# Two spectral-mixing and gated layers on one core: the order of down products, a staging buffer for row forms, and smaller issue pieces in the woven transforms

## The chip, the core and the metric

The kernel runs on one core of a Trainium2 chip. The metric is the time of one execution on the device, in microseconds; lower is better. Before the change the median of three runs is 1369.7 us (1366.79 to 1371.06).

## What is computed

An input x of 2048 rows by 512 columns, in float32, goes through two layers. Each layer has two residual steps: a spectral filter over both axes and a gated unit whose two branches are multiplied without a nonlinearity. Both begin with a layer normalization.

```python
x = x + irfft2(rfft2(layernorm(x)) * (w_r + 1j * w_i))
h = (layernorm(x) @ w_gate) * (layernorm(x) @ w_up)
x = x + h @ w_down
```

There are 2048 x 257 filter coefficients, and w_gate and w_up are 512 x 1792, w_down 1792 x 512; both layers use the same weights.

## The kernel before

**Data.** x stays in SBUF for the whole kernel as `xs`, 16 tiles of 128 x 512. A float32 operand that TensorE is to multiply at full accuracy in its reduced format is split into a high and a low part (`hi`/`lo`, `split`: a cast on ScalarE, then a subtraction), and one product becomes three matmuls, high x high, high x low, low x high (`mm3`, line 107).

**The stages of a layer.** A forward transform (`fwd_steps`, line 215) takes each tile through steps a0 (sums and differences, twiddle load), a1 (transposes), a2 (row transform) and a3 (column part into the buffer `E`). `mid_phase` does the rest of the column transform, the filter and the way back. `inv_steps` (line 382) brings each tile back by b0 (twiddle load), b1 (product `vp` out of `E`, split into `vs`) and b2 (twelve matmuls `yi`, three additions to xs, then the deviation for the next normalization). `stats` and `rstd` compute mean and deviation: `rstd` issues the square root on ScalarE and leaves four small VectorE operations in the list `small`, which `fill` issues at some later place.

**Forms.** The gated unit multiplies with a Strassen-like scheme in seven products, so it wants sums and differences of blocks, of the rows and of the weights. `build_x` (line 430) makes the row forms of a pair of tiles: `norm` (normalize), `turn` (four transposes into a bank `tq`, twice), `forms` (copies and sums, high and low parts of `XA`, three blocks, and of `XS`, four blocks). `XA` and `XS` hold 512 columns, that is one half of the rows. `beside` makes the weight forms (`wt`, from the loaded `rg`) of the next slice of 128 hidden columns on ScalarE and GpSimd, and the split of its down weights (`wd`, from `rw`), distributed over the seven products of the running unit by the list `names`.

**A unit** (`unit`, line 529) is one slice `ft` for one half of the rows (512 columns) or for half of that (256 columns, called a half unit here). Its products, in the order of issue, are p5 (bank `gw`), p1 (`gx`), p6 (`gy`), p2 (adds onto `gx`), p7 (`gz`), p3 (`gv`), p4 (adds onto `gz`): six matmuls each. VectorE combines the banks into c12 and c21, and `split` makes h of each, on ScalarE and GpSimd. The down products of a unit (`down`, three matmuls into one of two banks `db`, then an addition to xs on VectorE) are not issued in the unit itself but handed on as `prev` and issued between the products of the next unit: eight for a full unit, four for a half one. With the shares `(0, 0, 0, 3, 8, 8, 8)` of eight, three come after p2 and five after p7.

**Order.** From the first unit of a layer to the end of its last one, every engine executes instructions in the order of issue (`pin`, line 111). So the order in the program is the order of the queues: SyncE's for the loads of `rg`, `rw` and twiddles, GpSimd's for the low parts and sums, VectorE's and ScalarE's for everything that leaves a bank. `weave` (line 622) mixes a list `side` into a list `main`: each entry has a cost, and after each entry of main so many entries of side are issued that the shares of both sums keep pace, with the side ending at the fraction `frac` of main. Entries of main marked `hold` are followed by none. A side entry of cost 0 is issued together with the one before it as soon as its turn comes.

**One layer's gated units** (line 685 on), with the pinned order: half units (0, 1) of the first 256 columns with the rest of the inverse transform woven in; half units (0, 1) of the other 256 columns; the ten full units 2 to 11 with the second half's inverse (`inv2`) woven in; then half units 12 and 13, beside which the row forms of the second half replace those of the first in `XA` and `XS`, half by half; the ten full units 11 to 2 of the second half, in the first layer with the next forward transform (`fa`) woven in; half units 1 and 0.

**Buffers.** `E` (tag "e", one buffer) is read last by b1 of the last tile and written again by the next forward transform. The five buffers of tag "g" hold `rw`, `vs`, `xn`, `fo`, `fe`, `us` in turn, a new tenant waiting for the old one's last reader. PSUM has the banks x, y, w (one each), a (three: transforms and transposes) and d (two: down products).

## Time and profile before

| | |
|---|---|
| median of three runs | 1369.7 us (1366.79 to 1371.06) |
| the profiled execution, its time | 1371.37 us |
| its span, first to last instruction | 1369.6 us |
| busy in that span: TensorE matmuls | 1199.9 us (88%), 5804 instructions |
| weight loads (beside the matmuls) | 945.9 us (69%) |
| VectorE | 901.1 us (66%) |
| GpSimd | 765.3 us (56%) |
| ScalarE | 468.4 us (34%) |
| mean granted TensorE clock | 0.956 |

PE is TensorE, PEld its weight loads, DVE VectorE, ACT ScalarE, POOL GpSimd, SP SyncE. In a row of groups stand line, engine, operation, output and inputs by the program's names, shape and count, then busy time and mean duration in ns, then the idle time of the engine in front of them and what ended it. Line 123 is the helper that records every operation, so groups are told apart by their tiles. A busy PE is not PE at its peak, since the ends of matmuls are modelled; distances between starts are the safer measure. In rows of a timeline the first numbers are start and length in us, and brackets hold the idle time before.

### The profile page before, as it was taken

To read this page: it belongs to the slowest core of one execution; us is meant where nothing else is said; L and a number is where in the kernel's file an instruction comes from. 1 tells how busy PE (TensorE), PEld (TensorE's weight loads), DVE (VectorE), ACT (ScalarE), POOL (GpSimd) and SP (SyncE) were. 2 spreads that over 40 slices of the span, in tenths; PEclk is the share of its full clock that TensorE was granted. 3 is DMA by queue.
4 is the path that set the end of the run, shared out by engine and by line. 5 is a ranking of instruction groups with operands and counts; after the bars stand their busy time and mean duration, and the time that the engine had idled before them with its cause. 6 is when DMAs were issued, how large, how long until landed. Compare 5 with 4: busy or idle time off the path is not lost.

```text
span 1369.6 us, 16523 instructions
## 1 busy us (share of the span) xinstructions
PE 1199.9 (88%) x5804; PEld 945.9 (69%) x5804; DVE 901.1 (66%) x1669; ACT 468.4 (34%) x947; POOL 765.3 (56%) x804
## 2 busy tenths in 40 slices
PE   5888569999998978989989885699999989999998
PEld 4736557777777756777777365577777777777777
DVE  8568446666668776655576684466766687566666
ACT  5965223222322333333325652232222322322221
POOL 4443338655774655756651333385557745877772
PEclk9989789999999989999999897899999999999999
DMA  5531001111200010112104310011111012211011
GB/s 220 185 138 40 16 8 51 54 43 54 72 33 9 1 47 27 54 50 67 42 16 170 128 49 8 16 47 54 46 39 50 32 43 70 69 47 46 31 32 62
DMA packets 30754, 77.67 MB, mean 57 GB/s; under 512 B 3408, under 2 KB 11856, under 8 KB 28368
## 3 DMA queue, kind: packets, MB, share of 16 engines
q1 hardware_dynamic: 29952, 73.54, 15.8%
q0 software_dynamic: 288, 2.10, 0.5%
q8 instruction: 46, 0.75, 0.2%
q10 hardware_dynamic: 432, 0.98, 0.2%
q14 instruction: 36, 0.29, 0.1%
HBM read 72.42 MB, written 4.19 MB: 56 GB/s over the span
## 4 chain that ended last, share of the span: by engine, by line
PE 53%; DVE 22%; POOL 12%; issue 7%; ACT 4%; DMA 1%; POOLq 0%; SPq 0%; DVEq 0%; ACTq 0%
PE db L123 13%; DVE xs L123 10%; PE gx L123 9%; PE gz L123 8%; PE gw L123 4%; PE gy L123 4%; PE gv L123 4%; DVE q L123 3%; PE yi L123 3%; POOL wt L123 3%; PE dp L123 2%; POOL jz L123 2%; PE sp L123 2%; DVE st L123 2%; PE vp L123 2%
## 5 line engine op out<-in xcount | busy, mean ns | idle before, releaser
L123 PE MATMUL db<-wd,h 128*128 128x512 f32 x1344 | 378.1, 408 | 42.1 <-DVE xs L123 30.9
L123 DVE TENSOR_TENSOR xs<-xs,db 128x512 f32<-128x512 f32 x448 | 304.2, 685 | 106.6 <-PE db L123 105.9
L123 PEld LDWEIGHTS db<-wd,h 128*128 128x128 f32 x1344 | 235.2, 189 | 141.5 <-DVE xs L123 101.9
L123 POOL TENSOR_TENSOR wt<-rg,wt 128x512 fp32r<-128x512 f32 (+1 forms) x216 | 232.8, 1085 | 135.7 <-ACT wt L123 134.8
L123 POOL TENSOR_TENSOR h<-q,h 128x512 fp32r<-128x512 f32 (+1 forms) x144 | 167.9, 1185 | 167.5 <-ACT h L123 167.5
L123 PE MATMUL gx<-xA,wt 128*128 128x512 f32 (+1 forms) x864 | 189.2, 356 | 5.8 <-ACT s L123 5.6
L123 ACT CAST wt<-rg 128x512 fp32r<-128x512 f32 (+1 forms) x216 | 110.6, 539 | 183.3 <-POOL rg L123 168.4
L123 PEld LDWEIGHTS gx<-xA,wt 128*128 128x128 f32 x864 | 144.2, 197 | 28.5 <-ACT s L123 10.5
L123 ACT CAST h<-q 128x512 fp32r<-128x512 f32 (+1 forms) x144 | 75.6, 525 | 233.5 <-DVE q L123 232.6
L123 POOL TENSOR_TENSOR rg<-rg 128x256 f32<-128x256 f32 x200 | 147.6, 738 | 10.7
L123 PE MATMUL gw<-xS,wt 128*128 128x512 f32 (+1 forms) x432 | 97.6, 359 | 43.3 <-ACT xS L123 22.3
L123 DVE TENSOR_TENSOR q<-gy,s 128x512 f32<-128x512 f32 (+1 forms) x72 | 41.2, 572 | 139.9 <-PE gy L123 55.9
L123 POOL TENSOR_TENSOR wd<-rw,wd 128x512 fp32r<-128x512 f32 x52 | 69.0, 1328 | 85.7 <-ACT wd L123 85.7
L123 PEld LDWEIGHTS gw<-xS,wt 128*128 128x128 f32 x432 | 72.1, 195 | 60.4 <-ACT xS L123 23.9
L123 PE MATMUL gy<-xS,wt 128*128 128x512 f32 (+1 forms) x432 | 93.9, 355 | 0.0
L123 POOL TENSOR_TENSOR sx<-sx 128x256 f32<-128x256 f32 x64 | 47.7, 745 | 78.9 <-ACT sx L123 75.1
L123 PE MATMUL gz<-xS,wt 128*128 128x512 f32 (+1 forms) x432 | 90.8, 346 | 0.6 <-DVE q L123 0.6
L123 PE MATMUL gv<-xS,wt 128*128 128x512 f32 (+1 forms) x432 | 91.2, 347 | 0.0
L123 PE MATMUL gz<-xA,wt 128*128 128x512 f32 (+1 forms) x432 | 90.4, 346 | 0.0
L123 PEld LDWEIGHTS gz<-xS,wt 128*128 128x128 f32 x432 | 72.8, 190 | 13.9 <-DVE q L123 1.0
L123 PEld LDWEIGHTS gv<-xS,wt 128*128 128x128 f32 x432 | 72.9, 192 | 12.8
L123 PEld LDWEIGHTS gy<-xS,wt 128*128 128x128 f32 x432 | 73.0, 199 | 9.3
(88 smaller groups left out, 1619.0 us busy)
## 6 DMA issues: line engine op xcount, KB each, us to landing
rg<-in_wb_dram SPq DMA_DIRECT2D x50, 512.0 KB, 3.5
rw<-in_wb_dram SPq DMA_DIRECT2D x52, 256.0 KB, 2.6
wq<-in_wf_dram SPq DMA_DIRECT2D x10, 1024.0 KB, 4.8
wr<-in_wf_dram SPq DMA_DIRECT2D x6, 1024.0 KB, 5.6
tw<-in_tf_dram SPq DMA_DIRECT2D x32, 128.0 KB, 2.1
tw<-in_ti_dram SPq DMA_DIRECT2D x32, 128.0 KB, 2.1
out_dram<-xs SPq DMA_DIRECT2D x16, 256.0 KB, 2.0
xs<-in_x_dram SPq DMA_DIRECT2D x7, 512.0 KB, 7.9
```

The lines of the kernel that those rows point to most:

```text
L123: ins = f(*args, **kw)
```

## The change

Six things are changed.

- **Down products.** The shares become `(0, 0, 2, 4, 6, 8, 8)`: two downs each after p6, p2, p7 and p3 (one each in a unit that follows a half unit). Those after p3 are held like p3 itself. The split of c12 is issued after the downs behind p3 instead of inside p3, and the split of the down weights (`dh`, `dl`) after p4 instead of after p7.
- **Row forms of the second half.** `norm`, `turn` and the four sums are woven into the ten full units and the first half unit of slice 12, and written to a buffer `xf` of tag "e" (the place of `E`) of eight blocks for each pair; for the half units that follow, copies (`high`) and differences (`low_a`, `low_s`) from there into `XA` and `XS` remain. In layer 0 a new `E` is taken after that. The blocks of `XA` are in another order, with the products' indices to match.
- **Inverse.** b2's additions become entries b3 and b4 of their own, then `stats`, `rstd`, and its four small operations (`rest`) one step later; building of row forms starts one step later (`n + 4`), and the inverse's steps before the pinned order reach one further (`< 9`).
- **Forward.** `stats` and a0 get cost 0.2, and `rest` is an entry of its own, one step after `rstd`; `fill` is gone.
- **Weaves.** The fractions become 0.8 (from 1.0) for the first half units, 0.93 (from 0.7) for the long one, 0.6 (from 0.7) for the two that build row forms.
- **Half unit 12** of the first half belongs to the long weave.

```diff
@@ -176,28 +176,24 @@
...
 
-    small = []
-
-    def fill(n=1):
-        for _ in range(min(n, len(small))):
-            small.pop(0)()
-
     def rstd(nm):
...
         A.activation(q, var, AF.Sqrt, bias=eps)
-        small.extend([
-            lambda: V.reciprocal(r0, q),
-            lambda: stt(q, var, EPS, r0, op0=ALU.add, op1=ALU.mult),
-            lambda: stt(q, q, -0.5, r0, op0=ALU.mult, op1=ALU.mult),
-            lambda: stt(r, q, 1.5, r0, op0=ALU.add, op1=ALU.mult)])
+
+        def rest():
+            V.reciprocal(r0, q)
+            stt(q, var, EPS, r0, op0=ALU.add, op1=ALU.mult)
+            stt(q, q, -0.5, r0, op0=ALU.mult, op1=ALU.mult)
+            stt(r, q, 1.5, r0, op0=ALU.add, op1=ALU.mult)
+
+        nm["rest"] = rest
         nm["r"] = r
...
     def normed(t, nm):
-        fill(9)
         xn = temp("xn", "g")
@@ -231,7 +227,6 @@
...
             tt(fe[:, 1], fo[:, 2], fo[:, 3], ALU.subtract)
-            fill(9)
 
@@ -264,7 +259,6 @@
...
                 A.mul(u[64:128, jj, 1:256], dp[q, 257:512], r[q])
-                fill()
 
@@ -278,12 +272,13 @@
...
             ts = nms[t]["ts"]
-            ops.append((n, 4, 0, lambda t=t: stats(t, nms[t])))
+            ops.append((n, 4, 0.2, lambda t=t: stats(t, nms[t])))
             if t == ts[-1]:
                 ops.append((n, 5, 0, lambda t=t: rstd(nms[t])))
+                ops.append((n + 1, 5, 0.1, lambda t=t: nms[t]["rest"]()))
             i = ts.index(t)
             b = n - i + len(ts) + i
-            for d, f, o, c in ((0, a0, 3, 0), (1, a1, 2, 0.43), (2, a2, 6, 1.3), (4, a3, 1, 0.9)):
+            for d, f, o, c in ((0, a0, 3, 0.2), (1, a1, 2, 0.43), (2, a2, 6, 1.3), (4, a3, 1, 0.9)):
                 ops.append((b + d, o, c, lambda f=f, t=t: f(t)))
@@ -409,25 +404,33 @@
...
                         i == 0, i == 3)
-            xt = xs[:, t].rearrange("p (a d) -> p a d", a=2)
+            s["y"] = yp
+
+        def b3(t):
+            xt, yp = xs[:, t].rearrange("p (a d) -> p a d", a=2), S[t]["y"]
             tt(xt, xt, yp[:, None, 0:256].to_broadcast([128, 2, 256]), ALU.add)
+
+        def b4(t):
+            xt, yp = xs[:, t].rearrange("p (a d) -> p a d", a=2), S[t]["y"]
             tt(xt[:, 0], xt[:, 0], yp[:, 256:512], ALU.add)
             tt(xt[:, 1], xt[:, 1], yp[:, 256:512], ALU.subtract)
-            stats(t, nms[t])
-            if t == nms[t]["ts"][-1]:
-                rstd(nms[t])
-            s.clear()
+            S[t].clear()
 
...
         for n, t in enumerate(order):
-            for d, f, o, c in ((0, b0, 3, 0), (1, b1, 2, 1.0), (2, b2, 4, 1.42)):
+            nm = nms[t]
+            for d, f, o, c in ((0, b0, 3, 0), (1, b1, 2, 1.0), (2, b2, 4, 1.42), (2, b3, 5, 0.3), (2, b4, 6, 0.3)):
                 ops.append((n + d, o, c, lambda f=f, t=t: f(t)))
+            ops.append((n + 2, 7, 0.3, lambda t=t: stats(t, nms[t])))
+            if t == nm["ts"][-1]:
+                ops.append((n + 2, 8, 0, lambda nm=nm: rstd(nm)))
+                ops.append((n + 3, 3, 0.1, lambda nm=nm: nm["rest"]()))
             if build and n % 2:
-                for k, (c, f) in enumerate(build(nms[t])):
-                    ops.append((n + 3 + k // 2, 5 if k < 2 else 1, c, f))
+                for k, (c, f) in enumerate(build(nm)):
+                    ops.append((n + 4 + k // 2, 9, c, f))
         return in_steps(ops)
 
-    def build_x(X, nm, tags):
+    def build_x(X, nm, tags, stage=None):
 
@@ -443,24 +446,46 @@
...
             s[h] = tq.rearrange("p (b k s) -> p b k s", b=2, k=2)
+            if stage is not None:
+                A.copy(stage["t"][:, r, 2 - 2 * h:4 - 2 * h], s[h])
 
...
             A.copy(S[:, 0:2], b)
-            A.copy(XA[:, 0:2, 0, :, cols], a)
-            A.copy(XA[:, 2, 0, :, cols], b[:, 1])
+            A.copy(XA[:, 1:3, 0, :, cols], a)
+            A.copy(XA[:, 0, 0, :, cols], b[:, 1])
             gtt(S[:, 1], S[:, 0], S[:, 1], ALU.add)
...
             gtt(S[:, 3], S[:, 3], S[:, 2], ALU.subtract)
-            tt(XA[:, 0:2, 1, :, cols], a, f32(XA[:, 0:2, 0, :, cols]), ALU.subtract)
-            tt(XA[:, 2, 1, :, cols], b[:, 1], f32(XA[:, 2, 0, :, cols]), ALU.subtract)
+            tt(XA[:, 1:3, 1, :, cols], a, f32(XA[:, 1:3, 0, :, cols]), ALU.subtract)
+            tt(XA[:, 0, 1, :, cols], b[:, 1], f32(XA[:, 0, 0, :, cols]), ALU.subtract)
             A.copy(XS[:, :, 0, :, cols], S)
...
 
+        def sums():
+            G_ = stage["t"][:, r]
+            gtt(G_[:, 5], G_[:, 0], G_[:, 1], ALU.add)
+            gtt(G_[:, 4], G_[:, 2], G_[:, 0], ALU.subtract)
+            gtt(G_[:, 6], G_[:, 5], G_[:, 2], ALU.subtract)
+            gtt(G_[:, 7], G_[:, 3], G_[:, 6], ALU.subtract)
+
+        def high():
+            A.copy(XA[:, :, 0, :, cols], stage["t"][:, r, 1:4])
+            A.copy(XS[:, :, 0, :, cols], stage["t"][:, r, 4:8])
+
+        def low_a():
+            tt(XA[:, :, 1, :, cols], stage["t"][:, r, 1:4], f32(XA[:, :, 0, :, cols]), ALU.subtract)
+
+        def low_s(h):
+            gtt(XS[:, h:h + 2, 1, :, cols], stage["t"][:, r, 4 + h:6 + h], f32(XS[:, h:h + 2, 0, :, cols]), ALU.subtract)
+
+        if stage is not None:
+            return ([(0.2, norm), (0.43, lambda: turn(0)), (0.43, lambda: turn(1)), (0.3, sums)],
+                    [(0.5, high), (0.5, lambda: low_s(0)), (0.5, low_a), (0.5, lambda: low_s(2))])
         return [(0, norm), (0.43, lambda: turn(0)), (0.43, lambda: turn(1)), (0, forms)]
@@ -523,7 +548,7 @@
...
         names = ("start dstart", "h0 h12 l0 d0 h3 l3", "d1 l12 d2", "h5 l5 h4", "l4 d3 h6 l6 next", "dh", "dl") \
-            if eager else ("start dstart", "h0 h12 l0 d0", "l12 d1", "d2 d3 h34", "h56 l34 l56 next dh dl", "", "")
+            if eager else ("start dstart", "h0 h12 l0 d0", "l12 d1", "d2 d3 h34", "h56 l34 l56 next", "", "dh dl")
         return [[f[n] for n in g.split()] for g in names]
@@ -548,7 +573,7 @@
...
             box["x"] = bank("gx", "x")
-            prod(box["x"], 0, 0, True, True)
+            prod(box["x"], 1, 0, True, True)
             s1 = box["s1"] = new("s1")
@@ -565,7 +590,7 @@
...
         def p2():
-            prod(box["x"], 1, 2, False, True)
+            prod(box["x"], 2, 2, False, True)
 
@@ -587,10 +612,10 @@
...
             tt(c12, box["x"][:, :n], c12, ALU.mult)
-            split(0, c12)
+            box["c12"] = c12
 
         def p4():
-            prod(box["z"], 2, 6, False, True)
+            prod(box["z"], 0, 6, False, True)
             c21 = box["q"]
@@ -608,11 +633,14 @@
...
         for i, p in enumerate((p5, p1, p6, p2, p7, p3, p4)):
-            ops.append((c, p) if i < 5 else ("hold", c, p))
-            upto = len(prev) * (0, 0, 0, 3, 8, 8, 8)[i] // 8
-            ops += prev[done:upto]
+            hold = ("hold",) if i > 4 else ()
+            ops.append((*hold, c, p))
+            upto = len(prev) * (0, 0, 2, 4, 6, 8, 8)[i] // 8
+            ops += [(*hold, *o[-2:]) for o in prev[done:upto]]
             done = upto
-            ops += [(0, f) for f in (extra[i] if extra else ())]
+            if i == 5:
+                ops.append(("hold", 0, lambda: split(0, box["c12"])))
+            ops += [(*hold, 0, f) for f in (extra[i] if extra else ())]
         return ops, nxt
@@ -668,8 +696,8 @@
...
                          lambda nm: build_x(X, nm, ("d", "d") if nm["ts"][0] < 2 else ("a", "a")))
-        emit([o for o in inv1 if o[0] < 8])
-        rest = [o for o in inv1 if o[0] >= 8]
+        emit([o for o in inv1 if o[0] < 9])
+        rest = [o for o in inv1 if o[0] >= 9]
 
@@ -683,19 +711,23 @@
...
         pin["on"] = True
-        weave(units([(0, 0), (1, 0)], 0), rest)
+        weave(units([(0, 0), (1, 0)], 0), rest, 0.8)
         emit(units([(0, 1), (1, 1)], 0, {(1, 1): (2, True)}))
         inv2 = inv_steps(E, lambda: dcs["i"], nms, o2, busy, None)
-        weave(units([(ft, None) for ft in range(2, 12)], 0, {(ft, None): (ft + 1, False) for ft in range(2, 12)}), inv2, 0.7)
-        b1, b2 = [], []
-        for k, ts in enumerate(pairs[4:]):
-            (b1 if k < 2 else b2).extend(build_x(X, nms[ts[0]], ("a", "a")))
-        emit(units([(12, 0), (13, 0)], 0, {(12, 0): (13, True)}))
-        weave(units([(12, 1), (13, 1)], 0), b1, 0.7)
-        weave(units([(13, 0), (12, 0)], 8), b2, 0.7)
+        main = units([(ft, None) for ft in range(2, 12)] + [(12, 0)], 0,
+                     {(12, 0): (13, True), **{(ft, None): (ft + 1, False) for ft in range(2, 12)}})
+        stage = {}
+        both = [build_x(X, nms[ts[0]], ("a", "a"), stage) for ts in pairs[4:]]
+        inv2.append((0, lambda: stage.update(t=wk.tile([128, 4, 8, 2, 128], F32, name="xf", tag="e"))))
+        weave(main, inv2 + [o for pre, _ in both for o in pre], 0.93)
+        emit(units([(13, 0)], 0))
+        post = [[o for _, p in both[h:h + 2] for o in p] for h in (0, 2)]
+        weave(units([(12, 1), (13, 1)], 0), post[0], 0.6)
+        weave(units([(13, 0), (12, 0)], 8), post[1], 0.6)
         emit(units([(13, 1), (12, 1)], 8, {(12, 1): (11, True)}))
...
             dcs["f"] = load_df()
+            E = wk.tile([128, 16, 257, 2], F32, name="E", tag="e")
             g1 = [(0, 1), (2, 3), (4, 5), (6, 7)]
```

## Prediction

> **What bounds the kernel now.** I read the costliest groups first, then the chain of waits inside one undisturbed stage, then the busy times stage by stage.
>
> ```profile
> L123 PE MATMUL db<-wd,h 128*128 128x512 f32 x1344 | 378.1, 408 | 42.1 <-DVE xs L123 30.9
> L123 DVE TENSOR_TENSOR xs<-xs,db 128x512 f32<-128x512 f32 x448 | 304.2, 685 | 106.6 <-PE db L123 105.9
> ```
>
> TensorE waits 42.1 us in front of down products (db), 30.9 of them for VectorE's additions of finished ones (xs). That is only what shows as idle PE; the chain shows the mechanism. It is cut from the ten full units at the end of layer 1, where nothing else is woven in (columns: start, length, what).
>
> ```profile
> 1223.74 1.39 PE gv L123 x6
> 1225.13 1.36 PE gz L123 x6
> ...
> 1231.93 0.69 PE db L123 x3
> ...
> 1232.65 0.70 DVE xs L123
> ...
> 1233.39 0.97 PE db L123 x3
> ...
> 1236.46 0.69 DVE xs L123
> ...
> 1237.19 0.98 PE db L123 x3
> ...
> 1238.94 0.97 PE db L123 x3
> 1239.91 1.39 PE gv L123 x6
> ```
>
> A product of six 512-column matmuls takes 1.36 us, a down of three 0.68 (half of it). A unit is seven products and eight downs: 7 x 1.36 + 8 x 0.68 = 14.96. It repeats after 1239.91 - 1223.74 = 16.17. The 1.2 us more are the places where the chain leaves PE for DVE: downs come three and five in a row, there are two "d" banks, and an addition (0.69) is no shorter than a down, so the third of a run waits. The stages, as windows (us; then PE, PEld, DVE, ACT, POOL busy with counts, granted clock, DMA):
>
> ```profile
> 148.90:210.00 61.10, 44.01 (x253) 39.59 (x253) 29.06 (x65) 12.05 (x26) 22.37 (x23) 0.81 0.04 11
> 210.00:394.70 184.70, 174.72 (x810) 138.07 (x810) 121.74 (x195) 50.82 (x96) 119.04 (x115) 1.00 0.17 54
> 394.70:415.30 20.60, 19.91 (x121) 16.55 (x120) 14.81 (x27) 5.47 (x13) 13.55 (x15) 1.00 0.08 27
> 415.30:478.00 62.70, 54.07 (x358) 47.15 (x356) 48.40 (x99) 19.87 (x42) 36.20 (x38) 1.00 0.02 5
> 478.00:685.40 207.40, 183.72 (x778) 143.15 (x777) 127.91 (x207) 71.68 (x144) 126.42 (x131) 0.96 0.15 47
> 685.40:714.30 28.90, 28.12 (x175) 23.85 (x174) 20.45 (x38) 6.66 (x16) 15.12 (x17) 1.00 0.06 19
> 1164.10:1323.30 159.20, 156.03 (x649) 118.80 (x649) 100.32 (x147) 45.86 (x84) 118.90 (x115) 1.00 0.15 48
> ```
>
> I call them I (four half units beside the end of the inverse transform), II (ten full units, second half's inverse woven in), III (two half units), IV (six half units, building the second half's forms), V (ten full units of the second half; in layer 0 the next forward transform is woven in, in layer 1 nothing: last row), VI (three half units); between the layers and in front lie transforms. Layer 1 repeats I to IV to within 0.1 us. A half product costs the distance of two starts, 1155.02 - 1154.30 = 0.72:
>
> ```profile
> 1154.30 0.88 PE L123 MATMUL gv<-xS,wt 128*128 128x256 f32 x6
> 1155.02 0.88 PE L123 MATMUL gz<-xA,wt 128*128 128x256 f32 x6
> ```
>
> so a half unit is 7 x 0.72 + 4 x 0.68 = 7.76, with eight downs 10.48.
>
> **Downs two at a time.** Order after: p5, p1, p6, two downs, p2, two, p7, two, p3, two, p4. I lay it out by hand from a unit's start. gy ends at 4.08; DVE does q and q5 (0.69 each) to 5.5, the first two additions to 6.9. The first pair of downs runs 4.08 to 5.44, gx to 6.8: the third down needs the first addition, done at 6.2, a margin of 0.6; the fourth needs 6.9 and starts at 7.5. Later pairs have more room, since a pair (1.36) plus a product (1.36) stands against at most four DVE operations (2.8) whose results are needed a pair later. No down waits, and a plain unit comes to about 15.0: 1.2 gained. Stage V of layer 1: first unit 7 x 1.36 + 4 x 0.68 = 12.24, plus 9 x 14.96, is 146.9; 159.2 becomes 147.4, **-11.8**. VI: 10.48 + 2 x 7.76 = 26.0 of 28.9, **-2.8**, in each layer.
>
> What pays: downs begin one product earlier (after gy), and h's first split is issued after the pair behind p3, on POOL now behind the weight forms issued before it; wd's split moves to the unit's end. POOL's load over seven plain units:
>
> ```profile
> 1207.60:1320.70 113.10, 111.06 (x463) 84.61 (x462) 71.83 (x105) 31.64 (x56) 81.29 (x77) 1.00 0.13 42
> L123 POOL TENSOR_TENSOR h<-q,h 128x512 fp32r<-128x512 f32 x14 | 20.8, 1510 | 11.2 <-ACT h L123 11.2
> L123 POOL TENSOR_TENSOR rg<-rg 128x256 f32<-128x256 f32 x28 | 20.6, 737 | 1.6
> L123 POOL TENSOR_TENSOR wd<-rw,wd 128x512 fp32r<-128x512 f32 x7 | 9.1, 1295 | 19.0 <-ACT wd L123 19.0
> ```
>
> 81.29 / 7 = 11.6 us a unit, DVE 71.83 / 7 = 10.3, both under 14.96. The weight forms end near 12.5, the first h piece (1.51) then 0.9 after the unit's end, the second, behind p4's multiplication, near 3.6. The first down wants the first piece at 4.1, the fifth the second at 9.5. Margin 3.2 us: cost nothing; without that cover each us of POOL lag is one us a unit.
>
> **Inverse in pieces, stage II and III.** Tiles cost PE a yi and a vp each:
>
> ```profile
> 965.01 1.42 PE yi L123 x12
> 905.26 1.09 PE L123 MATMUL vp<-tw,E 128*128 128x128 f32 x8
> ```
>
> Floor of II: 146.9 + 8 x (1.42 + 1.09) = 167.0, waits 17.7; of III 10.48 + 7.76 = 18.2, waits 2.4. Today the three additions of a tile and its deviation stand on DVE in one lump before the db additions. In pieces they fit between, but the margin of 0.6 is gone where a piece (0.69 to 0.87) precedes a needed addition: I estimate 0.8 for eight units, 6.4. The staging moves in here: eight sets of transposes (an estimate of some 0.42 each, under twice the 0.23 of one 512-column matmul, as they move as many columns in four pieces; 3.4 in sum) and sixteen POOL sums. At 0.74, like the weight differences of equal size (rg), that is 12 us of POOL inside two units that leave it 14.96 - 11.6 = 3.4 each; then unit (12,0) makes the next weights early. By hand (13,0) starts with forms some 2 us late, twice, and with h late once: 5. Together 167.0 + 18.2 + 3.4 + 6.4 + 5 = 200 of 205.3, **-5**; bounds +8 (all 12 us of sums land on the path and the pieces gain nothing) to -14 (no wait is left but 3).
>
> **Building forms, IV.** Now:
>
> ```profile
> 1114.47 2.40 POOL L123 TENSOR_TENSOR xS<-sx,xS 128x1024 fp32r<-128x1024 f32 x1 [1.16 <-ACT xS L123]
> 1114.59 0.98 PE L123 MATMUL gw<-xS,wt 128*128 128x256 f32 x6 [1.49 <-DVE q L123]
> 1115.36 1.79 DVE L123 TENSOR_TENSOR q<-q,c 128x256 f32<-128x256 f32 x1
> L123 ACT CAST xS<-sx 128x1024 fp32r<-128x1024 f32 x16 | 16.7, 1047 | 41.0 <-POOL sx L123 41.0
> ```
>
> Transposes, normalization and sums leave this stage; left are copies from the stage buffer and differences, issued in the first 0.6. Floor 6 x 7.76 = 46.6. The two high copies of a pair (1.05 for the 1024 columns, somewhat less for the 768) stand on ACT before s1, which gx's second half waits for: about 1.2 in two units, 1 elsewhere: 50 of 62.7, **-12.5**; bounds -8 and -16. The Trainium skill, "SBUF — State Buffer", section "Who interferes with whom", says a VectorE instruction with two SBUF inputs contends with a GpSimd one that reads SBUF. The trace agrees: 1.79 for a q<-q,c beside POOL's 2.40. It speaks against the change, whose low part of XA now reads the stage and no longer PSUM; at 1.3 each (a POOL piece of 512), were all four exposed, IV would come to 55.
>
> The buffer itself: it takes E's place after the last vp has read E, and in layer 0 the new E waits for the last difference; both lie a unit or more before the first use, so nothing, or at most one unit's 15 if the copy into it came early.
>
> **Forward weave, stage V of layer 0.** Statistics and a0 had cost 0, so the whole head was issued at the first product:
>
> ```profile
> 479.23 0.68 DVE L123 BATCH_NORM_STATS2 st<-xs 128x6 f32<-128x512 f32 x1
> 485.42 0.69 PE L123 MATMUL tp<-midt,fo 128*128 128x128 f32 x2 [5.76 <-POOL fo L123]
> 499.22 0.98 PE L123 MATMUL db<-wd,h 128*128 128x512 f32 x3 [3.70 <-DVE xs L123]
> ...
> 612.26 1.47 PE L123 MATMUL dp<-df,fs 128*128 128x256 f32 x8
> 613.48 1.64 PE L123 MATMUL gx<-xA,wt 128*128 128x512 f32 x6
> 614.95 0.10 POOL L123 MEMSET us<- 64x4 f32 x1
> 617.18 1.65 PE L123 MATMUL gx<-xA,wt 128*128 128x512 f32 x6 [0.69 <-ACT s L123]
> 620.04 1.03 PE L123 MATMUL sp<-us,tw 128*128 128x257 f32 x4
> 620.72 1.05 PE L123 MATMUL db<-wd,h 128*128 128x512 f32 x3
> ```
>
> A tile costs PE 1.22 (dp, by starts), 0.68 (sp) and some 0.3 (tp, an estimate): floor 146.9 + 8 x 2.2 = 164.5, waits 42.9. With costs of 0.2 the head spreads over three products; I leave 1.5 for its first tp. Where dp falls on a unit's start, POOL's clearing of us stands behind h's second piece and now wd too, and ACT's s1 behind it: 1.1 in three units. The rest, 0.9 in each of ten units for DVE pieces in the way. 164.5 + 14 = 178.5, **-29**; bounds -18 (no more than the head and 0.6 a unit) and -38.
>
> **The first half units, I.**
>
> ```profile
> 874.98 0.58 PE L123 MATMUL gw<-xS,wt 128*128 128x256 f32 x1 [6.12 <-ACT xS L123]
> ```
>
> Floor 5.04 + 3 x 7.76 = 28.3 plus 2 yi, one vp and transposes, against 61.1 at a clock of 0.81. One tile's rear moves ahead of the first unit (its yi and vp, 2.5, take 5 at half clock, part of it under PE's wait for the first forms), its lump leaves unit (1,0), and the last forms are issued 2 us earlier against the 6.12. Net **-8**; bounds 0 and -14. The Trainium skill, "TensorE: Matmul & The Clock Gate", section "What's actually happening", has the clock halved after an idle window of about 3.4 us; the trace agrees (0.81 here, 1.00 in II). By it, removing the 6 us waits would add some 5 us to the gain.
>
> The transforms outside (reciprocal steps issued one step later instead of filled in) do the same operations: 0, bounds 5 either way.
>
> **Sum.** The profiled execution took 1371.4 (span 1369.6). Twice (8 + 5 + 12.5 + 2.8) = 56.6, plus 29 and 11.8: 97. It gives 1274; that execution lies 1.7 above the median of the runs, so **1272**.
>
> **Rivals.** *Only plain units gain.* Where anything is woven, the pieces queue as the lumps did: 11.8 (V, layer 1) + three plain units of II, 2 x 3.6, + III 4.8 + VI 5.6 + half units in IV 6 (0.5 each, from VI's 28.9 less 26.0 over three, rounded down) = 35: 1335. For it: DVE is 122 of 185 busy in II and the margin is 0.6; against: 42.9 us of V hang on one issue lump. *POOL late at the staging.* Sums and early weights push (12,0) and (13,0) back by the full 12: II and III +8, so 13 more in each layer, 1298; for it POOL's 119.0 of 184.7 already. *Slower: POOL becomes the bound.* Place: h's first piece behind the weight forms, which the first pair of downs waits for. It decides once POOL is more than 3.2 us late in every unit, that is when its 11.6 a unit grow past 14.96; the whole gain is gone at 14.96 + 97 / 56 = 16.7, and at 17.5 it is 56 x 2.5 - 97 = 43 over: 1415. For it h's 1.51 against 1.29 for wd of the same size; against: 11.6 would have to grow by half.
>
> **Chances.** Forecast 0.70, plain units only 0.13, staging 0.12, POOL the bound 0.05. The range 1240 to 1315 holds the first and third with the bounds of their terms and leaves out the others, 0.18. A measurement here tells apart about 0.3% (4 us). Faster 0.95, same 0.01, slower 0.04, from the last rival.
>
> **What would show it.** Right: units of layer 1's V repeat every 15.0, no DVE xs in front of db there; stage IV near 50 with no 2.4 us POOL piece; V of layer 0 without tp's 5.8 and db's 3.7; I at 53. Wrong: db waiting for h or POOL, gx for ACT s1 above 1 us a unit, or (13,0) waiting for wt by more than 5. The forecast fails as a whole if plain units stay at 16.2.

## The result, and the profile after

The changed kernel takes 1271.56 us (median of three runs, 1267.3 to 1273.38) against 1369.7: a ratio of 0.9281, 95% interval 0.9237 to 0.9325. Forecast was 1272. The profiled execution has a span of 1265.5, 104.1 less than before; the medians differ by 98.1, since the execution profiled before lay 1.7 above its median and this one 4.3 below.

The costliest groups of the changed kernel (busy time, mean ns, idle time of the engine in front and what ended it):

```profile
L123 PE MATMUL db<-wd,h 128*128 128x512 f32 x1344 | 367.5, 399 | 10.2 <-ACT h L123 4.0
L123 DVE TENSOR_TENSOR xs<-xs,db 128x512 f32<-128x512 f32 x448 | 297.0, 681 | 49.0 <-PE db L123 48.8
```

TensorE's idle time in front of downs fell from 42.1 to 10.2, and its main releaser is no longer the addition on VectorE. A plain unit in layer 1's stage V shows why (timeline of TensorE; start, length; x6 is one product or two downs):

```profile
1146.54 1.52 PE L123 MATMUL gw<-xS,wt 128*128 128x512 f32 x6
...
1149.26 1.52 PE L123 MATMUL gy<-xS,wt 128*128 128x512 f32 x6
1150.62 1.52 PE L123 MATMUL db<-wd,h 128*128 128x512 f32 x6
1151.97 1.52 PE L123 MATMUL gx<-xA,wt 128*128 128x512 f32 x6
1153.34 1.52 PE L123 MATMUL db<-wd,h 128*128 128x512 f32 x6
...
1161.49 1.52 PE L123 MATMUL gw<-xS,wt 128*128 128x512 f32 x6
```

Every start lies 1.35 to 1.37 behind the one ahead, without a bracket, and the unit repeats after 1161.49 - 1146.54 = 14.95. The stages of layer 1 (I to V, in their order), and ahead of them stage V of layer 0 (us; PE, PEld, DVE, ACT, POOL busy; granted clock, DMA):

```profile
453.10:626.40 173.30, 170.06 (x778) 140.10 (x777) 125.55 (x207) 70.22 (x144) 122.43 (x132) 1.00 0.18 55
...
770.70:820.80 50.10, 36.85 (x232) 33.90 (x233) 25.17 (x56) 11.14 (x24) 22.09 (x23) 0.83 0.04 12
820.80:998.50 177.70, 171.57 (x839) 142.81 (x838) 125.69 (x219) 54.02 (x103) 124.48 (x128) 1.00 0.16 51
998.50:1023.10 24.60, 21.34 (x126) 18.44 (x125) 14.23 (x27) 5.99 (x15) 16.68 (x20) 0.93 0.24 75
1023.10:1072.20 49.10, 47.77 (x327) 43.56 (x326) 37.90 (x71) 14.32 (x29) 23.87 (x26) 1.00 0.12 44
1072.20:1221.30 149.10, 147.62 (x649) 121.34 (x649) 97.05 (x147) 45.26 (x84) 114.82 (x116) 1.00 0.16 51
```

The large gains are V of layer 0 (207.4 to 173.3), IV (62.7 to 49.1), I (61.1 to 50.1) and V of layer 1 (159.2 to 149.1). II fell by 7, and III grew from 20.6 to 24.6. What TensorE still waits for in II and III (timeline, only rows with a wait in front):

```profile
968.83 0.63 PE L123 MATMUL tq<-midt,xn 128*128 128x128 f32 x4 [2.63 <-DVE xn L123]
...
981.23 1.09 PE L123 MATMUL tq<-midt,xn 128*128 128x128 f32 x8 [1.70 <-DVE xn L123]
...
993.21 0.63 PE L123 MATMUL tq<-midt,xn 128*128 128x128 f32 x4 [1.02 <-DVE xn L123]
...
1012.43 0.50 PE L123 MATMUL gy<-xS,wt 128*128 128x256 f32 x2 [0.71 <-ACT wt L123]
...
1015.35 0.75 PE L123 MATMUL db<-wd,h 128*128 128x512 f32 x2 [1.38 <-ACT h L123]
```

The first three are the staging's own transposes, which stand in TensorE's order before their normalization is done. The last two belong to (13,0), half unit 13 of the first 256 columns, whose weights and h are late on ScalarE and POOL. So the staging is where something is paid back; the experiments measure how much.

### The profile page after: what moved, and what is told of

The parts are those of the page before. It is cut to its first block, busy times and chain, and to the rows that moved or that the text cites. A ratio compares the mean times of both kernels' runs of the same rounds, so it can differ in the third digit from the quotient of the medians.

```text
span 1265.5 us, 16593 instructions
## 1 busy us (share of the span) xinstructions
PE 1146.9 (91%) x5804; PEld 943.0 (75%) x5804; DVE 880.9 (70%) x1661; ACT 461.6 (36%) x939; POOL 749.7 (59%) x812
## 4 chain that ended last, share of the span: by engine, by line
PE 35%; POOL 14%; issue 6%; DVE 5%; ACT 2%; DMA 1%; POOLq 0%; DVEq 0%; ACTq 0%
PE db L123 11%; PE gz L123 5%; PE gx L123 5%; POOL wt L123 5%; POOL rg L123 3%; PE gw L123 3%; PE gy L123 3%; PE gv L123 3%; POOL h L123 2%; PE dp L123 2%; DVE xs L123 1%; DVE q L123 1%; POOL jz L123 1%; PE sp L123 1%; PE yi L123 1%
## 5 line engine op out<-in xcount | busy, mean ns | idle before, releaser
L123 PE MATMUL db<-wd,h 128*128 128x512 f32 x1344 | 367.5, 399 | 10.2 <-ACT h L123 4.0
L123 DVE TENSOR_TENSOR xs<-xs,db 128x512 f32<-128x512 f32 x448 | 297.0, 681 | 49.0 <-PE db L123 48.8
L123 POOL TENSOR_TENSOR h<-q,h 128x512 fp32r<-128x512 f32 (+1 forms) x144 | 151.6, 1057 | 251.4 <-ACT h L123 169.4
L123 PEld LDWEIGHTS db<-wd,h 128*128 128x128 f32 x1344 | 244.5, 191 | 62.6 <-DVE xs L123 9.3
L123 PE MATMUL gx<-xA,wt 128*128 128x512 f32 (+1 forms) x864 | 185.0, 351 | 2.7 <-ACT s L123 2.7
L123 POOL TENSOR_TENSOR rg<-rg 128x256 f32<-128x256 f32 x200 | 149.0, 745 | 10.9
L123 PE MATMUL gw<-xS,wt 128*128 128x512 f32 (+1 forms) x432 | 94.8, 354 | 32.1 <-ACT xS L123 22.2
L123 PEld LDWEIGHTS gz<-xA,wt 128*128 128x128 f32 x432 | 72.1, 188 | 12.0
L123 ACT ACTIVATE us<-dp,rs 64x257 f32<-64x257 f32 (+1 forms) x128 | 60.3, 471 | 36.2 <-PE dp L123 29.9
```

The lines of the kernel that those rows point to most:

```text
L123: ins = f(*args, **kw)
```

## Experiments

The stages of the main runs, each profiled execution cut at the starts of the gw that open a stage (us; layer 0 / layer 1; "between" runs from the end of VI of layer 0, that is from the start of unit (0,1), to I of layer 1; "tail" is what follows VI in layer 1):

| stage | before | after | e1 pairs only | e2 old downs | e3 no staging | e7 last sums late |
|---|---|---|---|---|---|---|
| start | 148.9 | 148.2 | 145.2 | 148.8 | 147.2 | 147.9 |
| I | 61.1 / 61.2 | 51.0 / 50.1 | 57.0 / 57.3 | 52.2 / 51.6 | 50.0 / 50.6 | 50.8 / 50.2 |
| II | 184.7 / 184.7 | 179.1 / 177.6 | 171.6 / 171.6 | 196.4 / 196.4 | 169.1 / 168.5 | 176.1 / 175.6 |
| III | 20.6 / 20.6 | 25.6 / 24.6 | 20.6 / 20.6 | 24.6 / 24.8 | 20.6 / 20.6 | 22.7 / 22.9 |
| IV | 62.7 / 62.7 | 49.1 / 49.1 | 62.8 / 62.8 | 53.6 / 53.4 | 62.6 / 62.6 | 49.0 / 49.0 |
| V | 207.4 / 159.3 | 173.3 / 149.2 | 197.0 / 149.1 | 189.1 / 159.5 | 173.4 / 149.3 | 173.5 / 149.2 |
| VI | 28.9 / 28.9 | 28.4 / 28.4 | 28.4 / 28.4 | 28.9 / 28.9 | 28.4 / 28.4 | 28.4 / 28.4 |
| between | 120.6 | 115.9 | 117.6 | 114.9 | 116.5 | 114.8 |
| tail | 17.4 | 15.8 | 15.8 | 17.1 | 15.8 | 15.8 |
| span | 1369.6 | 1265.5 | 1305.8 | 1340.0 | 1263.4 | 1254.2 |

Stages that an edit doesn't touch repeat to within 1 to 2 us, "between" to within some 2 and "start" to within some 4 (145.2 to 149.0). "Early forms" are the weight forms that a half unit makes for the unit right behind it (the first list of `names`); "pieces" are the split-up steps of the woven transforms, "pairs" the downs two at a time.

### e1: the pairs alone, on the kernel before

```diff
-            ops.append((c, p) if i < 5 else ("hold", c, p))
-            upto = len(prev) * (0, 0, 0, 3, 8, 8, 8)[i] // 8
+            hold = ("hold",) if i > 4 else ()
+            ops.append((*hold, c, p))
+            upto = len(prev) * (0, 0, 2, 4, 6, 8, 8)[i] // 8
...
+            if i == 5:
+                ops.append(("hold", 0, lambda: split(0, box["c12"])))
```

(and `dh dl` at the unit's end.)

> The kernel before with one part of the change alone: downs two at a time, c12's split behind the last pair, wd's split at the unit's end. Theory (pairs cure only the two-bank wait, lumps stay): layer 1's stage V 159.2 -> about 148 and units of 15.0; three plain units of II in each layer, III, VI and IV gain as well, some 30 us in all: 1340; V of layer 0 stays above 195, with tp's 5.8 and db's 3.7 still there. Rival (pairs also give the woven units their 1.2 each): 7 more units of II twice and 10 of V in layer 0, some 28 us more: about 1312. Rival (POOL is late with h): V of layer 1 not under 157.

1308.45 us, ratio 0.9569 (0.954 to 0.9598). The rival holds for the woven units. That the total came so near its 1312 is partly luck: of the half units among its 30, those of III and IV gained nothing and VI 0.5, while I gained 4 a layer, and the stretch before the first unit, which the edit doesn't touch, is 3.7 shorter. Stage II and both stages V:

```profile
202.20:373.90 171.70, 168.37 (x811) 140.11 (x810) 119.52 (x195) 49.86 (x96) 114.74 (x116) 1.00 0.19 57
457.20:654.20 197.00, 178.33 (x778) 144.02 (x777) 124.86 (x207) 71.15 (x144) 121.93 (x132) 0.96 0.16 50
1112.50:1261.60 149.10, 147.58 (x650) 121.54 (x649) 97.16 (x147) 45.35 (x84) 114.97 (x116) 1.00 0.17 51
```

II gains 13.1 in each layer, as much a unit (1.3) as a plain unit, although the inverse's lumps are still issued whole: in layer 1's II all of TensorE's waits for xs come to 2.0 us. A product between two pairs seems to give VectorE room for a lump too. In layer 0's V the pairs gain 10.4, and the waits at the lump stay, 6.15 us of tp and 3.13 of db. Half units gain in I (4 a layer), not in III and IV.

### e2: the changed kernel with the old places of the downs

The diff of e1 turned round.

> The changed kernel with the old places of the downs (three behind p2, five behind p7, c12's split inside p3, wd's split at p7); pieces and staging stay. Theory (parts add up): layer 1's V back to about 160, the whole some 30 us above the changed kernel, about 1302. Rival (pieces pay only together with pairs, since a piece in front of a db addition stalls a run of five): II and layer 0's V lose more than 1.2 a unit, 45 to 70 us above, 1317 to 1340.

1344.42 us, ratio 0.9832 (0.9802 to 0.9862): 74.5 of span above the changed kernel. The rival holds again, at 4 us over its upper end. II goes up by 17 and 19, past that of the kernel before. What stands in front of its downs (timeline):

```profile
889.88 0.97 PE L123 MATMUL db<-wd,h 128*128 128x512 f32 x3 [0.91 <-DVE xs L123]
...
895.92 1.65 PE L123 MATMUL db<-wd,h 128*128 128x512 f32 x6 [0.66 <-DVE xs L123]
```

In runs of three and five, downs wait for VectorE in these units although its work comes in pieces. Of the 11.7 by which II is longer than before, the staging makes 9 to 10 (e3), so by this subtraction pieces without pairs gave II nothing. IV, too, is some 4.4 shorter with pairs once the staging has emptied it, although e1 found nothing for them there. The parts don't simply add, and the subtraction above is an argument for the same reason.

### e3: no staging

```diff
-        weave(main, inv2 + [o for pre, _ in both for o in pre], 0.93)
-        emit(units([(13, 0)], 0))
-        post = [[o for _, p in both[h:h + 2] for o in p] for h in (0, 2)]
-        weave(units([(12, 1), (13, 1)], 0), post[0], 0.6)
-        weave(units([(13, 0), (12, 0)], 8), post[1], 0.6)
+        weave(units([(ft, None) for ft in range(2, 12)], 0, {...}), inv2, 0.7)
...
+        emit(units([(12, 0), (13, 0)], 0, {(12, 0): (13, True)}))
+        weave(units([(12, 1), (13, 1)], 0), b1, 0.7)
+        weave(units([(13, 0), (12, 0)], 8), b2, 0.7)
```

> The changed kernel without the staging: forms of the second 1024 rows built inside IV as before, the rest as changed. Theory (staging only moved cost: IV's 13 us a layer are paid back in II and III as transposes, waits of tq for xn and a late start of (13,0)): IV 58 to 62, II+III 190 to 194, total 1266 to 1276. Rival (the prediction's terms): IV +12.5 less some 3 that the pairs give, II+III -8.4, so +1 to +4 a layer and, with (13,0) at 8 instead of 13, not below 1272: 1274 to 1280.

1266.18 us, ratio 0.9264 (0.9236 to 0.9292), which can't be told from the change's 0.9281 (0.9237 to 0.9325). The first theory holds. Stages II, III and IV of layer 1:

```profile
818.20:986.70 168.50, 167.35 (x810) 140.31 (x809) 122.61 (x211) 50.48 (x96) 114.99 (x116) 1.00 0.17 53
986.70:1007.30 20.60, 19.17 (x121) 16.79 (x121) 14.44 (x27) 5.41 (x14) 14.11 (x16) 1.00 0.09 34
1007.30:1070.00 62.70, 55.63 (x359) 50.12 (x358) 47.74 (x83) 19.25 (x41) 36.00 (x38) 0.95 0.16 55
```

Without staging II is 168.5, 1.5 above its floor of 167.0, and III 20.6; with it they are 177.6 and 24.6. It takes 13.5 out of IV (62.6 less 49.1) and puts 13.1 into II and III of layer 1 (202.2 less 189.1), 15.0 in layer 0 (204.7 less 189.7). The whole staging, as built, moved time and saved none.

### e4: the forward transform's head as a lump again

```diff
-            ops.append((n, 4, 0.2, lambda t=t: stats(t, nms[t])))
+            ops.append((n, 4, 0, lambda t=t: stats(t, nms[t])))
...
-            for d, f, o, c in ((0, a0, 3, 0.2), (1, a1, 2, 0.43), (2, a2, 6, 1.3), (4, a3, 1, 0.9)):
+            for d, f, o, c in ((0, a0, 3, 0), (1, a1, 2, 0.43), (2, a2, 6, 1.3), (4, a3, 1, 0.9)):
```

> The changed kernel with the forward transform's statistics and a0 at cost 0 again, so that they are issued in one lump at the first product of stage V in layer 0. Theory (the lump was worth the 5.8 and 3.7 and some of the waits behind): V of layer 0 173 -> 183 to 191, total 1281 to 1290. Rival (pairs alone removed the waits, the lump is hidden now): V of layer 0 under 177, total within 4 us of 1271.6.

1289.01 us, ratio 0.9427 (0.9391 to 0.9462); V of layer 0 is 192.7 instead of 173.3. The first theory holds, 1.7 over its range for the stage. TensorE's waits in it:

```profile
459.94 0.69 PE L123 MATMUL tp<-midt,fo 128*128 128x128 f32 x2 [4.90 <-POOL fo L123]
...
509.38 2.61 PE L123 MATMUL db<-wd,h 128*128 128x512 f32 x6 [2.42 <-DVE xs L123]
...
551.69 0.96 PE L123 MATMUL db<-wd,h 128*128 128x512 f32 x3 [1.74 <-DVE xs L123]
```

In the changed kernel the wait of tp is 0.79, and of waits for xs there is one, of 1.48.

### e5: the early weight forms' differences on VectorE

```diff
-            gtt(box["r"][:, o], box["r"][:, a], box["r"][:, b], ALU.subtract)
+            (tt if dv else gtt)(box["r"][:, o], box["r"][:, a], box["r"][:, b], ALU.subtract)
```

(`dv` is set for the early forms only.)

> The changed kernel with the four differences of the early weight forms ((13,0)'s, ft 0's, ft 2's and ft 11's next weights, made within one half unit) on VectorE instead of POOL: 3.0 us of POOL less in each of four half units a layer. Theory (POOL and ACT, passing these forms to and fro, make h late there): VI 28.4 -> about 26.5, III 25 -> about 22, total 1260 to 1265. Rival (VectorE, 20.1 of VI's 28.4 busy, then holds up db): waits of db for xs take the place, total within 4 us of 1271.6 or above.

1279.31 us, ratio 0.9352 (0.933 to 0.9375): slower, as the rival had it, but not for VectorE's load. VectorE and TensorE at the start of VI in layer 1 (from two timelines of e5):

```profile
1237.65 0.42 DVE L123 TENSOR_TENSOR rg<-rg 128x256 f32<-128x256 f32 x1 [4.06 <-POOL wt L123]
1237.99 0.42 DVE L123 TENSOR_TENSOR q<-gy,s 128x256 f32<-128x256 f32 x1
...
1238.78 1.28 DVE L123 TENSOR_TENSOR xs<-xs,db 128x512 f32<-128x512 f32 x2
```

```profile
1239.52 2.17 PE L123 MATMUL db<-wd,h 128*128 128x512 f32 x6 [3.13 <-DVE xs L123]
...
1247.47 0.88 PE L123 MATMUL gw<-xS,wt 128*128 128x256 f32 x6
...
1255.26 0.88 PE L123 MATMUL gw<-xS,wt 128*128 128x256 f32 x6
```

The difference takes 0.42 there instead of 0.74, but it overwrites the raw block that POOL still reads. So VectorE stands 4.06 us, with q and the db additions queued behind, and TensorE 3.13. One thing came out as the theory had it: unit (0,0), 9.4 us in the changed kernel, takes 1255.26 - 1247.47 = 7.79, its floor. With (1,0) ahead of it at 15.5 instead of 11.18 the forms had the time they lack in the changed kernel, which agrees with their late end as the cause of its excess.

### e6: normalizations earlier, and e7: the last sums later

```diff
-        weave(main, inv2 + [o for pre, _ in both for o in pre], 0.93)
+        weave(main, inv2[:-3] + seq[:1] + inv2[-3:] + seq[1:], 0.93)
```

`seq` holds the staging's entries with each `norm` moved before the second `turn` of the pair ahead.

> The changed kernel with each normalization of the staging issued before the second transposes of the pair ahead, the first before the last three steps of the inverse. Theory (TensorE's in-order waits of tq for xn, 2.6 + 1.7 + 1.0 in a layer, are lost time): II 178 -> about 173, total 1259 to 1265. Rival (the wait only moves, to the weights of (13,0) that POOL finishes late): II shorter and III longer by the same, total 1268 to 1272.

1265.0 us, ratio 0.9247 (0.9222 to 0.9271), an interval that overlaps the change's. By the stages it lies between the two: II is 6.1 and 4.5 shorter, III 2.6 and 3.6 longer. Of the three waits of tq one of 0.87 is left, and a new one opens (12,0):

```profile
961.71 0.63 PE L123 MATMUL tq<-midt,xn 128*128 128x128 f32 x4 [0.87 <-DVE xn L123]
...
992.04 0.74 PE L123 MATMUL gw<-xS,wt 128*128 128x256 f32 x4 [3.08 <-POOL wt L123]
```

Sums that now start earlier stand ahead of the weight forms on POOL (four of them, 3.33 us from 987.43, and the awaited forms right behind). e7 is the changed kernel, without e6's edit, and takes the last pair's sums out of that queue:

```diff
+        weave(main, inv2 + [o for pre, _ in both for o in pre][:-1], 0.93)
...
+        post[0].append(both[3][0][-1])
```

> The changed kernel with the last pair's four sums (2.9 us of POOL, now inside (12,0) ahead of the early weight forms) issued in IV beside the first half units. Theory (POOL's backlog makes (13,0) 13 instead of 7.8): III 25 -> about 22, IV unchanged at 49, total 1264 to 1268. Rival (the to and fro of ACT and POOL over the seven pieces sets (13,0)'s start): III 24 to 25, IV up to 3 longer, total 1270 to 1278.

1256.76 us, ratio 0.9194 (0.9173 to 0.9215): better than forecast, and faster than the change by an interval that doesn't touch the change's. II, III and IV of layer 1:

```profile
813.30:988.90 175.60, 171.64 (x835) 142.13 (x834) 124.33 (x219) 53.47 (x102) 121.28 (x126) 1.00 0.16 47
988.90:1011.80 22.90, 20.20 (x130) 17.79 (x129) 14.26 (x27) 6.56 (x16) 17.24 (x18) 1.00 0.35 115
1011.80:1060.70 48.90, 47.70 (x326) 43.49 (x325) 37.65 (x71) 14.34 (x29) 26.75 (x30) 1.00 0.12 44
```

POOL's 2.9 us moved into IV (23.87 busy to 26.75), which didn't grow; III gave back 1.7 (3.0 in layer 0) and II 2.0 (3.0). III's part is the theory's: (13,0) takes 10.1 to 10.3 for 13.0 to 14.0, (12,0) 0.9 more than in the changed kernel. II's part was not forecast, and it goes with VectorE's normalizations rather than with POOL's queue: the staging's transposes wait 2.1 us for them in a layer instead of 5.4. The entry that is missing changes the weave's spacing from II's first unit on (15.1 for 14.2 in layer 1), so the transposes are issued at other places.

```profile
961.70 0.63 PE L123 MATMUL tq<-midt,xn 128*128 128x128 f32 x4 [0.53 <-DVE xn L123]
...
971.72 1.08 PE L123 MATMUL tq<-midt,xn 128*128 128x128 f32 x8 [0.70 <-DVE xn L123]
...
977.78 0.63 PE L123 MATMUL tq<-midt,xn 128*128 128x128 f32 x4 [0.86 <-DVE xn L123]
```

Its median is the lowest of all versions.

### e8: the moved tile's rear put back

```diff
-        emit([o for o in inv1 if o[0] < 9])
-        rest = [o for o in inv1 if o[0] >= 9]
+        first = lambda o: o[0] < 8 or o[:2] == (8, 9)
+        emit([o for o in inv1 if first(o)])
+        rest = [o for o in inv1 if not first(o)]
```

> The changed kernel with the inverse steps of one more tile taken back behind the first half unit; the forms of the second pair stay ahead of it. Theory (that tile's rear is hidden under PE's wait for the first forms): the stretch between the layers stays at 116, I is 3 to 6 longer in each layer, total 1277 to 1283. Rival (the prediction's: the rear costs about 5 ahead of the first unit): the stretch between the layers shrinks by as much as I grows, total within 4 us of 1271.6.

1278.01 us, ratio 0.9354 (0.9328 to 0.938). The first theory holds. The stretch between the layers, then I of layer 1:

```profile
656.00:772.00 116.00, 91.63 (x418) 62.99 (x416) 89.32 (x198) 66.32 (x135) 41.78 (x50) 0.91 0.28 104
772.00:828.40 56.40, 43.33 (x252) 39.74 (x253) 28.65 (x65) 11.72 (x25) 22.08 (x23) 0.79 0.05 13
```

The first is 116.0 with or without that tile (the changed kernel, with that tile's matmuls in it, has 115.9); I is 6.3 longer, 4.2 in layer 0. So ahead of the first unit the rear costs less than the some 2 us by which that stretch varies. It fills the wait of a set of transposes for its normalization, 5.48 us in e8 and 1.50 in the changed kernel (layer 1); the wait for the first forms behind it is the same with it or without (5.23 and 5.03).

### e9 and e10: POOL's load raised in stage V of layer 1

```diff
-            if eager else ("start dstart", "h0 h12 l0 d0", "l12 d1", "d2 d3 h34", ...
+            if eager else ("start dstart", "h0 h12 l0 d0", "l12 " + more * "l12 " + "d1", "d2 d3 h34", ...
```

(`more` is 2 in e9, 4 in e10.)

> The changed kernel with POOL's work of a unit raised in stage V of layer 1 alone: one 512-column weight low part is made three times instead of once, 2.6 us more of POOL a unit (11.5 -> 14.1, still under 14.96). Theory (POOL's lag is free up to 3.2 us): V of layer 1 at 149 to 150. Rival (h stands behind the weight forms, so each us of lag shows at once): 2.6 a unit, V at 170 or more.

> As the one before with five times instead of once: 5.2 us more of POOL a unit, 16.7 against 14.96. Theory (POOL is the bound past the unit's length, after a lag of some 3 us is used up): 10 x 1.7 less 3, V of layer 1 at 149 + 14 = 161 to 166, with units of 16.7 and db waiting for POOL's h. Rival (POOL is off the path at any load of this size): V at 149 to 151.

e9: 1275.73 us, ratio 0.9333 (0.9302 to 0.9363); e10: 1300.38, 0.9501 (0.9477 to 0.9524). Stage V of layer 1 in e9 is 154.3 and in e10 178.7:

```profile
1067.00:1221.30 154.30, 150.41 (x650) 122.81 (x649) 100.70 (x147) 44.73 (x84) 139.75 (x134) 0.98 0.15 47
```

```profile
1071.80:1250.50 178.70, 158.26 (x651) 124.90 (x650) 97.94 (x147) 43.70 (x83) 166.42 (x154) 0.95 0.13 40
```

e9 lies between its theory and its rival. The two first units take 5.1 more than in the changed kernel (15.1 and 19.3 for 12.9 and 16.4) and the eight others 15.0 again: at 14.1 a unit POOL is free, apart from a start at which it is behind with the early forms, which the theory had left out. In e10 the units take 16.5 to 19.0, on average 17.8, over POOL's 16.7: the theory's mechanism, but dearer than its 161 to 166. What ends the waits there (waits over that stage: engine, releaser, us in total, times, longest):

```profile
ACT wt L123 <- POOL rg L123: 102.5, 22, 8.8
...
ACT wt L123 <- DMA rg<-in_wb_dram: 14.7, 10, 2.8
PE gw L123 <- POOL wt L123: 12.5, 9, 1.9
...
PE gw L123 <- ACT wt L123: 7.6, 5, 5.3
...
PE db L123 <- POOL h L123: 0.4, 1, 0.4
```

It isn't h that comes late but the next unit's weights, at gw; in the changed kernel that wait came once, 1.1 us. The raw weights have one buffer: the next load starts when POOL has read the last block, so a late POOL also waits for the load behind it. That, and a clock of 0.95, fit the 1.1 us a unit beyond POOL's own work; their shares were not told apart.

### e11: the early forms in another order, and e12: all three

```diff
-        names = ("start dstart", "h0 h12 l0 d0 h3 l3", "d1 l12 d2", "h5 l5 h4", "l4 d3 h6 l6 next", "dh", "dl") \
+        names = ("start dstart", "h0 h12 l0 d0 h3 l3", "d1 l12 d2", "h5 l5 h4", "l4 d3", "", "h6 l6 next dh dl") \
```

> The changed kernel with the early weight forms issued in another order: the last piece (ACT's copy that waits for POOL's difference, and its low part) and wd's split behind the splits of h, nothing added or left out. Theory (ACT's split of h queues behind that copy in its own queue): (0,0) 9.4 -> about 8, VI 28.4 -> 26.5 to 27.2, III a little shorter, total 1262 to 1267. Rival (the to and fro of POOL and ACT over seven pieces is too long for a half unit in any order): VI 28 or more, total within 4 us of 1271.6.

1267.91 us, ratio 0.9258 (0.9235 to 0.9281), which can't be told from the change's. VI is 27.45, between the two; III is 1 to 2 shorter. The first full units of V give it back: V of layer 1 is 151.8 for 149.2, and the gw of its second unit waits 0.79 for ScalarE's and 1.79 for POOL's weights, where the changed kernel has 1.13 for POOL's alone.

> The changed kernel with early normalizations, the sums of the last two pairs issued in IV, and the early forms in the other order. Theory (three separate causes, gains add): II 173, III 21 to 22, IV 49 to 50, VI about 27, total 1246 to 1252. Rival (POOL's work only moves, so that IV pays for II and III): IV 52 or more, total 1254 to 1260.

(e12 also moves the sums of the last two pairs to IV, not of one.) 1260.22 us, ratio 0.9205 (0.9185 to 0.9225). Both theories missed: IV stayed at 48.9, VI is 27.4, but II is 174.9 and 176.5 instead of 173, and V is 2.9 and 2.7 longer, in layer 1 as in e11. Moving entries changes the costs by which the weave spaces all others; that II's gain was lost to this spacing is an argument, not shown. e12 is no better than e7 alone; their intervals overlap.

## Why the prediction was right, and where not

- **Plain units, V of layer 1 (-11.8).** Right: units of 14.95; the stage gained 10.1. The 1.7 missing are in its first two units (12.9 and 16.4 for 12.24 and 14.96; the second's gw waits 1.13 for weights). In e5, where the unit ahead is 2.0 longer, they take 12.34 and 14.96 and the stage 147.0, so the early forms' late end is what is missing.
- **VI (-2.8).** Mis-sized: -0.5. The step "10.48 + 2 x 7.76 = 26.0" left out the weight forms of ft 0, made within unit (1,0): (1,0) takes 11.18 and (0,0) 9.41. Before the change (0,0) took 8.32; pairs ask for h one product earlier, and here h is late. ScalarE and TensorE of the changed kernel in (0,0), from its timeline:

```profile
1234.70 0.41 ACT L123 CAST wt<-rg 128x256 fp32r<-128x256 f32 x1 [2.11 <-POOL rg L123]
1235.01 0.40 ACT L123 CAST h<-q 128x256 fp32r<-128x256 f32 x1
...
1235.46 0.73 PE L123 MATMUL db<-wd,h 128*128 128x512 f32 x2 [0.63 <-ACT h L123]
```

  ScalarE's split of h stood behind a copy of weights that waited 2.11 for POOL. It is the place that the slower rival named for full units, found in half units. e5 brings (0,0) to its floor, and e11's other order takes 0.94 of its excess of 1.65 away; the 0.7 of (1,0) was not followed up.
- **II and III (-5).** The sum was near (-0.6 and -3.1) by errors that cancel. The wait left beside the pieces, 6.4, was too high: 1.5 in e3 (2.0 in layer 0). III's own 2.4 of waits were taken as gone, and III without staging stays at 20.6: it has the two units of VI, with early forms between them (11.19 and 9.40). The staging, 3.4 + 5, was too low: 13 to 15. What was missed there is TensorE's own order: transposes issued next to their normalization wait for it, 5.4 us in a layer. And the pairs give 13.1 in II by themselves, where the prediction's working laid the relief of the woven units on the pieces; these add 2.6 to 3.1 (e1 to e3).
- **IV (-12.5).** Right: -13.6. The contention that spoke against it shows, but hidden: the low part of XA (128x768) took 1.67 where POOL's second piece of 1.3 was already running, and 0.94 where POOL began 0.3 before its end, in all four pairs of the two layers:

```profile
1026.47 2.55 POOL L123 TENSOR_TENSOR xS<-xf,xS 128x512 fp32r<-128x512 f32 x2 [0.95 <-ACT xS L123]
...
1028.16 1.67 DVE L123 TENSOR_TENSOR xA<-xf,xA 128x768 fp32r<-128x768 f32 x1
...
1033.69 0.94 DVE L123 TENSOR_TENSOR xA<-xf,xA 128x768 fp32r<-128x768 f32 x1
```

  This bears out the rule of the Trainium skill ("SBUF — State Buffer", "Who interferes with whom"); of an effect on the stage, up to 55 by the prediction, nothing shows at 49.1.
- **V of layer 0 (-29).** The mechanism was right and its size low: -34.1. Pairs alone give 10.4 (e1), and the spread head is worth 19.4 beside them (e4); the 4.3 left of the 34.1 were not told apart.
- **I (-8).** -10.1 and -11.0, near in sum and not in its terms. The pairs give 4 of it (e1), which no term had. The rear's 5 ahead of the first unit was a wrong term: no cost shows there, and moving it is worth 4 to 6 (e8). The last forms' 2 us hardly came: the wait of 6.12 is still 5.80 in the changed kernel, so nothing here tests what its removal would give.
- **Transforms (0).** The stretch between the layers gained 4.7, near the bound of 5. In e1, which leaves the reciprocal steps as they were, it is 3.0 shorter too, and it varies by as much among the others; what makes it stays open. The tail's 1.6 came with the pairs (e1).
- **The rivals.** "Only plain units gain" put the pairs alone at 1335; e1 gave 1308. "POOL late at the staging" came true in a small way: III is 4 to 5 longer. "POOL becomes the bound" put its threshold near the unit's length of 14.96; the runs have it between 14.1 and 16.7 a unit (e9, e10), and the wait is for weights and not for h.
- **The total.** That 1272 met 1271.6 to half a us is luck. By spans, II and III gave 6.3 less than forecast, VI 4.6 and V of layer 1 1.7; transforms and tail gave 7.0 more, I and V of layer 0 5.1 each, IV 2.2. That leaves some 7 us of span beyond the forecast, and it is where the two profiled executions lie among their runs that brings the medians together.

By spans, the 104.1 are 63.8 with the pairs (before to e1), 42.4 with the pieces and the moved rear on top of them (e1 to e3), and -2.1 with the staging (e3 to after). Of the 63.8, 3.7 lie before the first unit and 3.0 between the layers, where no cause was shown; the units and the tail account for the other 57.

## What to carry to other kernels

With few output banks, spread the matmuls whose results another engine must fetch between longer products, in runs no longer than the number of banks (here two banks and runs of two against three and five; no other number was run). That paid in plain and woven full units alike, not in every half unit, and without it finer pieces on the fetching engine left stage II no shorter. Work moved out of a slow stage is only gained if each in-order queue of the receiving stage has room at that place: here the average load of POOL left room, the last unit before the early weight forms did not, and 2.9 us of sums a layer, moved back out, were worth 1.7 to 3.0 a layer in III (e7). Transposes belong far enough behind their normalization: 5.4 us a layer in the changed kernel went into waits for it.

## What the runs showed of the hardware beyond expectation

- A shorter instruction on a faster engine lost: 0.42 instead of 0.74 for a difference, and 1279.3 against 1271.6 us in all, since the queue behind it was the one that TensorE waits for.
- Past POOL's capacity a unit costs more than POOL's work: 17.8 against 16.7, with the granted clock at 0.95.
- A set of transposes that takes some 0.4 us from its start to the next down's held TensorE for 2.63 us, with the downs queued behind it.
